# A list-scheduled attention and MLP kernel given a fixed order found by annealing, with one user at a time per PSUM bank and warm-up matmuls on a memset tile

## The chip, the cores and the metric

One core of a Trainium2 chip. Times are device microseconds (us) of one execution; where several executions were made, the median is given. The kernel before took 156.56 us (156.51 to 156.72, three runs). A profiled execution also has a **span**, from its first to its last instruction, about 2 us shorter than its time.

An execution can fall into a slower state, in which it takes over 1.5% longer than the fastest of the same kernel. Profiles whose execution was slow are named as such.

Engine names are those of the profile: PE does matmuls, DVE is the vector engine, ACT the scalar engine, POOL is GpSimd, SP issues most of the DMAs.

## The reference

An RWKV-style linear attention with a decaying state, then a LayerNorm and a two-layer MLP with a residual. Batch 4, 8 heads, 768 steps, head size 48; so 3072 rows of 384, which the kernel handles as 24 tiles of 128 rows.

```python
for t in range(S):                                   # per batch and head, D = 48
    cur   = einsum('bhd,bhe->bhde', u * k[t], v[t])
    y[t]  = einsum('bhd,bhde->bhe', r[t], state + cur)
    state = w * state + einsum('bhd,bhe->bhde', k[t], v[t])
x  = y, heads side by side                           # (4, 768, 384)
xn = (x - mean) / sqrt(var + 1e-6) * g_ln
out = x + maximum(xn @ w_ch1, 0) @ w_ch2             # 384 -> 1536 -> 384
```

## The kernel before

Each tile is a chain of some 20 tasks over all engines. r and k are scaled by powers of w on DVE or POOL (`scr`, `sck`), turned by PE (`TR`, `TK`) and evacuated by ACT or DVE (`rT`, `kT`). PE multiplies them (`at`), DVE masks (`A`), PE forms the bonus (`q`, `cc`, `cp`, `Vb`) and the state (`kv`, `S`, `Z`), then `y`. DVE adds (`x`), ACT or DVE centres (`xn`), the tile is turned (`ln`, `lc`, by PE for the first eight tiles and by DMA later), and PE does the MLP in pieces: three or six `up` with a relu each (`re`), three `dn`, then `ot` and the store `st`. The weights are scaled and cast on the way (`w1s`, `w2s`). `turn`, `vec`, `uw`, `wl` and `WLZ` prepare the decay and bonus vectors once.

A planner in the program walks these tasks with guessed costs and decides the order and, where there is a choice, the engine. Every engine then executes its own list in order.

```python
class Planner:
    def order(self, ...):
        ...
        while todo:
            for t in todo:                      # earliest start wins, then priority
                ...
                for eng, cost in [(t["eng"], t["cost"])] + (... t["alt"] or []):
                    ready = max(data, eng_at[eng] if eng else 0.0)
        ...
# (cut) one pool of PSUM, one bank per name, two for "hp":
#       at=1 (two banks), tr=1, s=1, y=1, hp=2, o=1
warm = ps.tile([P, 512], FP32, name="o")

def keep_warm(n):                               # matmuls that compute nothing
    for _ in range(n):
        nc.tensor.matmul(out=warm[:, :P], lhsT=ident[:], rhs=ident[:], start=True, stop=True)

def ln_transposes(i):
    ...
    tp_t[i] = ps.tile([P, 2 * HP, P], BF16, name="tr")     # shared with r and k transposes
    for kc in range(CK):
        nc.tensor.transpose(out=tp_t[i][:, kc, :], in_=xn_t[i][:, kc * P : (kc + 1) * P], identity=ident[:])
...
for t in plan.order():
    if t["eng"] == "PE":
        gap = t["start"] - pe_at - 0.1
        if gap > 0 and 0 not in o_t:            # where the plan leaves PE idle early on
            keep_warm(int(gap / 0.057))
        pe_at = t["start"] + t["cost"]
    ...                                         # emit t on the engine chosen
```

## Time and profile before

The profile that the prediction works from fell in the slow state. The kernel before was profiled again later, in a fast execution, with the same sources.

| kernel before | first profile (slow) | profiled again (fast) |
|---|---|---|
| time, us | 161.39 | 156.47 |
| span, us | 159.4 | 154.4 |
| mean granted PE clock | 0.989 | 1.000 |
| second half of `y` of tile 8 starts, us | 54.2 | 53.1 |
| end of PE, us | 156.15 | 151.15 |

How to read it: the activity rows give each engine's busy share in tenths, in 40 equal slices. The PE timeline gives the start of each group of matmuls, its length, and in brackets how long PE stood before it and for whom. The number to carry is the **lag**: the time at some place of the program less the useful PE work that stands before it (matmuls that the result needs, at full clock). It can only grow. Its last value, plus the 129 us of useful work and a tail after PE of some 3.25 us, is the span.

### The profile page before, as it was taken

To read this page: it belongs to the slowest core of one execution; us is meant where nothing else is said; L and a number is where in the kernel's file an instruction comes from. 1 tells how busy PE (TensorE), PEld (TensorE's weight loads), DVE (VectorE), ACT (ScalarE), POOL (GpSimd) and SP (SyncE) were. 2 spreads that over 40 slices of the span, in tenths; PEclk is the share of its full clock that TensorE was granted. 3 is DMA by queue.
4 is the path that set the end of the run, shared out by engine and by line. 5 is a ranking of instruction groups with operands and counts; after the bars stand their busy time and mean duration, and the time that the engine had idled before them with its cause. 6 is when DMAs were issued, how large, how long until landed. Compare 5 with 4: busy or idle time off the path is not lost.

```text
span 159.4 us, 4730 instructions
## 1 busy us (share of the span) xinstructions
PE 150.5 (94%) x1902; PEld 120.0 (75%) x1902; DVE 120.6 (76%) x246; ACT 94.2 (59%) x205; POOL 84.8 (53%) x115
## 2 busy tenths in 40 slices
PE   5999998999999999999999599999999999999991
PEld 5889887978887777677778367778787877777671
DVE  5879679699999999998899747779896965211142
ACT  3465787687868777677768444766767343354100
POOL 7387649486469857977988361874223622000000
PEclk9999999999999999999999968999999999999999
DMA  4999989998989998999586896211212122111122
GB/s 95 231 217 327 354 171 271 370 228 169 248 209 204 242 263 171 238 194 270 115 189 135 189 193 179 66 46 51 54 52 72 29 74 78 49 49 49 53 99 99
DMA packets 75563, 25.48 MB, mean 160 GB/s; under 512 B 69648, under 2 KB 74390, under 8 KB 75542
## 3 DMA queue, kind: packets, MB, share of 16 engines
q1 hardware_dynamic: 73542, 23.90, 62.1%
q10 hardware_dynamic: 1904, 1.28, 2.5%
q8 instruction: 15, 0.25, 0.6%
q14 instruction: 6, 0.05, 0.1%
q0 software_dynamic: 96, 0.01, 0.1%
HBM read 18.88 MB, written 4.72 MB: 148 GB/s over the span
## 4 chain that ended last, share of the span: by engine, by line
PE 55%; DVE 14%; SPq 14%; DMA 10%; issue 3%; ACT 1%; DVEq 0%; ACTq 0%
PE o L676 21%; PE hp L649 20%; SPq L212 9%; DMA wst<-in_moe_w_ch_dram 5%; DVE A L454 3%; DMA xT<-xn 3%; SPq L206 3%; PE at L444 2%; DMA k<-in_k_dram 2%; PE y L547 2%; PE tr L420 2%; PE tr L405 2%; DVE Z L519 2%; PE y L535 1%; SPq L234 1%
## 5 line engine op out<-in xcount | busy, mean ns | idle before, releaser
L649 PE MATMUL hp<-xT,w_sb 128*128 128x256 bf16 (+1 forms) x540 | 58.4, 253 | 2.4 <-DMA xT<-xn 2.0
L676 PE MATMUL o<-w_sb,hT 128*128 128x384 bf16 x264 | 52.9, 329 | 0.0
L663 ACT ACTIVATE hT<-hp 128x512 bf16<-128x512 f32 x62 | 36.5, 595 | 26.7 <-PE hp L649 26.1
L649 PEld LDWEIGHTS <-w_sb 128*128 128x128 bf16 x540 | 43.7, 98 | 10.5 <-DMA xT<-xn 2.4
L676 PEld LDWEIGHTS <-hT 128*128 128x128 bf16 x276 | 25.6, 98 | 11.9 <-issue 0.3
L454 DVE TENSOR_TENSOR A<-at,mask 128x1024 bf16<-128x1024 f32 x24 | 29.1, 1213 | 3.1 <-PE at L444 3.1
L479 POOL TENSOR_TENSOR Vb<-v,cc 128x384 f32<-128x384 f32 x24 | 21.2, 882 | 14.6 <-ACT cc L475 7.5
L686 DVE SCALAR_TENSOR_TENSOR ot<-o,rs,x 128x384 f32<-128x384 f32 x22 | 13.4, 610 | 16.2 <-PE o L676 16.0
L390 POOL TENSOR_TENSOR sc<-r,Fr 128x384 bf16<-128x384 f32 x15 | 16.3, 1094 | 4.1 <-DVE Fr L330 3.0
L387 POOL TENSOR_TENSOR sc<-k,Fk 128x384 bf16<-128x384 f32 x16 | 17.2, 1077 | 0.0
L587 ACT ACTIVATE sq<-x,sum 128x384 bf16<-128x384 f32 x24 | 14.7, 611 | 4.3 <-DVE x L560 3.1
L285 PE MATMUL o<-ident 128*128 128x128 bf16 x191 | 14.9, 236 | 1.6 <-DVE ident L260 1.6
L409 ACT COPY kT<-tr 128x512 bf16<-128x512 bf16 x22 | 12.8, 584 | 4.6 <-PE tr L405 2.7
L560 DVE SCALAR_TENSOR_TENSOR x<-y,Vb 128x384 f32<-128x384 f32 x24 | 13.1, 546 | 2.8 <-PE y L547 2.7
L285 PEld LDWEIGHTS <-ident 128*128 128x128 bf16 x191 | 12.7, 107 | 1.9 <-DVE ident L260 1.6
L426 ACT COPY rT<-tr 128x512 bf16<-128x512 bf16 x16 | 11.2, 738 | 2.9 <-PE tr L420 2.8
L598 POOL TENSOR_SCALAR rs<-sqs 128x2 f32<-128x2 f32 x12 | 2.5, 210 | 18.2 <-ACT sq L587 17.9
L574 DVE TENSOR_SCALAR xn<-x,sum 128x384 bf16<-128x384 f32 x17 | 10.0, 586 | 0.1
L405 PE MATMUL tr<-ident,sc 128*128 128x128 bf16 x92 | 9.1, 222 | 0.8 <-POOL sc L387 0.4
L444 PE MATMUL at<-rT,kT 48*128 48x128 bf16 x192 | 9.5, 218 | 0.3 <-ACT kT L409 0.2
L665 DVE TENSOR_SCALAR hT<-hp 128x512 bf16<-128x512 f32 x10 | 6.9, 685 | 3.0 <-PE hp L649 2.9
L601 POOL TENSOR_TENSOR rs<-rs,expo 128x2 f32<-128x2 f32 x12 | 8.6, 713 | 1.0
(93 smaller groups left out, 204.9 us busy)
## 6 DMA issues: line engine op xcount, KB each, us to landing
r<-in_r_dram SPq DMA_DIRECT2D x12, 384.0 KB, 4.9
k<-in_k_dram SPq DMA_DIRECT2D x24, 192.0 KB, 4.4
wst<-in_moe_w_ch_dram SPq DMA_DIRECT2D x6, 768.0 KB, 7.8
v<-in_v_dram SPq DMA_DIRECT2D x23, 192.0 KB, 4.2
out_dram<-ot SPq DMA_DIRECT2D x18, 192.0 KB, 2.2
out_dram<-ot ACTq DMA_DIRECT2D x5, 192.0 KB, 1.9
xT<-xn SPq DMA_TRANSPOSE x16, 2.6
v<-in_v_dram ACTq DMA_DIRECT2D x1, 192.0 KB, 3.8
```

Of the source, the lines that this page charges most:

```text
L212: eng.dma_start(out=dst[:], in_=src[b, :, s0 : s0 + L, :].rearrange("h t d -> t h d"))
L285: nc.tensor.matmul(out=warm[:, :P], lhsT=ident[:], rhs=ident[:], start=True, stop=True)
L387: eng.tensor_tensor(out=k_bufs[i % NSC][:, :, :D], in0=k_t[i][:], in1=Fk[:], op=ALU.mult)
L390: eng.tensor_tensor(out=r_bufs[e % NSR][:, j, :, :D], in0=r_t[e][:, :, j * D : (j + 1) * D], in1=Fr[:, j], op=ALU.mult)
L454: nc.vector.tensor_tensor(out=A_t[i][:].rearrange("p e q t -> p (e q) t"), in0=at_t[i][:].rearrange("p e q t -> p (e q) t"), in1=mask[:].u ...
L479: nc.gpsimd.tensor_tensor(out=Vb_t[i][:], in0=vf_t[i][:], in1=cc_t[i][:].unsqueeze(2).to_broadcast([P, H, D]), op=ALU.mult)
L560: nc.vector.scalar_tensor_tensor(out=x_t[i][:], in0=y_t[i][:, :C], scalar=1.0, in1=Vb_t[i][:].rearrange("p h d -> p (h d)"), op0=ALU.mult, ...
L587: nc.scalar.activation(out=sq[:], in_=x_t[i][:], func=ACT.Square, bias=sum_t[i][:], scale=-float(C), accum_out=sq_t[e][:, c : c + 1],)
L649: nc.tensor.matmul(out=hp[:, f * gw : (f + 1) * gw], lhsT=w1_sb[:, n, kc, fb * P : (fb + 1) * P], rhs=xT_t[g][:, kc, :gw], start=(kc == 0) ...
L663: nc.scalar.activation(out=out, in_=src, func=ACT.Relu)
L676: nc.tensor.matmul(out=o_t[i][:, :C], lhsT=hT_t[g][:, fk, j * P : (j + 1) * P], rhs=w2_sb[:, fk, :], start=(fk == 0), stop=(fk == FK - 1),)
L686: nc.vector.scalar_tensor_tensor(out=ot_t[i][:], in0=o_t[i][:, :C], scalar=rs_t[i // 2][:, i % 2 : i % 2 + 1], in1=x_t[i][:], op0=ALU.mult ...
```

## The change

The planner is no longer asked. A fixed list, found offline by annealing, gives the order of all tasks and the engine of each (`.A`, `.V`, `.G`, `.S` for ACT, DVE, POOL and SP; `*n` for n warm-up matmuls). The search modelled each PSUM bank as held by one user at a time. The transposes of the first four normalised tiles move from bank "tr" to bank "o". Warm-ups read a tile that DVE sets first of all, and the loads of r, k, v and the weights that had a choice between SP and ACT are all issued by SP. The intent is fewer waits in the first 50 us.

```diff
-SHIFT = { ... }                               # nudges for the planner
+ORDER = """
+r1 k1 k2 Fr0.V k3 v1 v2 w1l2 Fr1.A Fk.A w1l0 scr00.V scr10.G scr11.G r2 scr01.V *18 TR0 rT0.A sck0.V *1 TK0 kT0.A
+*1 turn vec uw.V rT1.A sck1.V vc0.V sck2.G *13 at0 *3 TK1 q0.V wl A0 *6 cc0 *1 kv0 kT1.A q1.G WLZ gn TR1 rT2.A *2
+y0 at1 rT3.A vc1.A cp0.V Vb0 Z0 sck3.G v3 A1 w1l1 TK2 kT2.V vc2.A cc1 cp1.A kv1 at2 x0 y1 xn0.A ln0 Vb1 q2.G Z1
+... (40 more rows)
+"""
     # (cut) Planner.order() now reads ORDER and only checks that each task follows what it needs
+    busy = const.tile([P, P], BF16, name="busy")
+    nc.vector.memset(busy[:], 1.0)
     ...
-            nc.tensor.matmul(out=warm[:, :P], lhsT=ident[:], rhs=ident[:], start=True, stop=True)
+            nc.tensor.matmul(out=warm[:, :P], lhsT=busy[:], rhs=busy[:], start=True, stop=True)
-    keep_warm(12)
+    keep_warm(18)
+    LNO = 4
+    def ln_bank(i):
+        return "o" if i < LNO else "tr"
     ...
-        tp_t[i] = ps.tile([P, 2 * HP, P], BF16, name="tr")
+        tl_t[i] = ps.tile([P, 2 * HP, P], BF16, name=ln_bank(i))
     # (cut) loads lose their choice of ACT; buffer reuse is written as explicit needs
-        gap = t["start"] - pe_at - 0.1         # no filling of gaps by the emission loop
-        ...
+        if "warm" in t:
+            keep_warm(t["warm"])
```

## The prediction

> **What bounds the kernel now.** I read the page first, then the PE timeline, then the DVE and DMA-queue timelines of the stretches that came out as limits.
>
> ```profile
> PE   5999998999999999999999599999999999999991
> ...
> DVE  5879679699999999998899747779896965211142
> ...
> PEclk9999999999999999999999968999999999999999
> DMA  4999989998989998999586896211212122111122
> ```
>
> Each digit is one fortieth of the span (4 us). PE looks full from the start, yet the row hides three things: warm-up matmuls, modelled overlaps, and one hole at slice 23 with a drop of the granted clock behind it. DVE is at 9 between slices 8 and 18 (32 to 76 us), and the DMA engines are full until about 90 us. The chain of waits says the same: DVE instructions carry it from 45 to 66 us, and from 92 us on it is PE alone, instruction after instruction. So there is a DVE-paced first half and a PE-paced second half.
>
> ```profile
> L649 PE MATMUL hp<-xT,w_sb 128*128 128x256 bf16 (+1 forms) x540 | 58.4, 253 | 2.4 <-DMA xT<-xn 2.0
> L676 PE MATMUL o<-w_sb,hT 128*128 128x384 bf16 x264 | 52.9, 329 | 0.0
> ...
> L454 DVE TENSOR_TENSOR A<-at,mask 128x1024 bf16<-128x1024 f32 x24 | 29.1, 1213 | 3.1 <-PE at L444 3.1
> ...
> L285 PE MATMUL o<-ident 128*128 128x128 bf16 x191 | 14.9, 236 | 1.6 <-DVE ident L260 1.6
> ```
>
> (The groups by line.) L285 is the 191 warm-up matmuls; they compute nothing. To see what PE really has to do I took starts of neighbouring pieces in the PE timeline: an "up" piece costs 0.66 us, a "down" piece 0.65, an r transpose 0.445, a k transpose 0.22, scores 0.33, bonus 0.105, state 0.17, y 0.20 and 0.17 more with carried state, an ln transpose 0.17, a half "down" 0.33. Times their counts (72, 69, 12, 24, 24, 24, about 24, 24/20, 8, 6): **129 us of useful PE work**. In this trace PE's useful work runs from 8.4 to 156.15 us. Define PE's **lag** at a moment as the time less the useful work already done; its final value sets the end.
>
> ```profile
> 27.94 0.33 PE L535 MATMUL y<-Z,rT 128*128 128x96 bf16 x4
> ...
> 45.62 0.36 PE L547 MATMUL y<-vv,A 128*128 128x48 bf16 x8
> ...
> 86.18 0.33 PE L535 MATMUL y<-Z,rT 128*128 128x96 bf16 x4
> ...
> 91.69 0.83 PE L649 MATMUL hp<-xT,w_sb 128*128 128x256 bf16 x6 [2.00 <-DMA xT<-xn]
> ...
> 93.40 1.49 PE L676 MATMUL o<-w_sb,hT 128*128 128x384 bf16 x4
> ```
>
> These are y of tiles 3, 6 and 15, then the hole and a "down" piece at half clock (0.65 us normally). Useful work before them in the order of the program: 10.6, 26.0, 64.4 us. Lag: **17.3, 19.6, 21.8**, and 27.1 at the end. Of the last 5.3, 2.0 is the wait and about 1.7 the half clock up to 96.7 us. This profiled run was slow (161.39 us, span 159.4, so 2.0 between the two); a fast run of 156.56 has a span of about 154.6, and a lag near 22.5. So nearly all lag is made **before 46 us**, not in the dense part.
>
> What makes it there: DVE. The same count for DVE (row means, less 0.05 us for the overlap of neighbours, since their sum exceeds the busy time by that) gives 35.0 us before y6 and 74.4 before y15. Time less DVE work: 8.9 at y3, 10.6 at y6, 11.8 at y15. DVE thus lost 2 to 3 us of waits up to y6, then hardly any.
>
> ```profile
> 16.73 0.48 DVE L371 TENSOR_SCALAR w_sb<-wst,g_neg 128x512 bf16<-128x512 f32 x1 [0.46 <-DMA wst<-in_moe_w_ch_dram]
> ...
> 20.68 0.74 DVE L426 COPY rT<-tr 128x512 bf16<-128x512 bf16 x1 [1.01 <-ACT rT L426]
> ...
> 31.50 0.36 DVE L381 CAST w_sb<-wst 128x384 bf16<-128x384 f32 x1 [1.37 <-DMA wst<-in_moe_w_ch_dram]
> ```
>
> (DVE timeline.) DVE, first in first out, stands at weight pieces that have not landed, and at one half of the r evacuation until ACT has read the other half of the same bank.
>
> **What the Trainium skill says.** *PSUM — Partial Sum Buffer*, section "PSUM bank collisions raise a hardware error", says two engines may not be in one bank and quadrant together, so software must order them. The trace agrees: DVE rT waits for ACT rT 3.1 us in 5 places. *SBUF — State Buffer*, "Who interferes with whom": a DVE instruction with two SBUF inputs contends with a GpSimd one that reads SBUF. The trace agrees: the same k scaling on DVE takes 1.14 us at 7.25, while GpSimd scales, and 0.54 at 40 us when GpSimd idles. *TensorE: Matmul & The Clock Gate*, "What's actually happening": PE starts at half clock and is released by activity. Warm-up matmuls start about 0.115 us apart at 1.61 us here and 0.057 later. *Perfetto Trace Analysis*, "Identifying the Most-Contended Engine", warns that matmul busy share misleads; here 94% stands over 129 useful us of 159.
>
> **The change part by part.**
> *Warm-ups.* 191 become 73 (in the built kernel: 18, 10 and 18 before the first r transposes, 27 later): 118 fewer at 0.057 is 6.7 us of PE time. But they filled waits, so alone they give at most the few tenths by which a useful piece stood behind one. The memset tile lets the first warm-up start about 0.5 us sooner; the start-up chain to the first transposes is DVE scans and PE table transposes, so 0 to 0.2 us.
> *Work per engine.* Useful PE work unchanged. DVE 119.3 to 116.7 us by row means, ACT 102 to 98, GpSimd 84 to 91. r evacuations on DVE fall from 8 to 4, xn from 17 to 12; relus on DVE rise from 10 to 18.
> *The order.* Useful PE / DVE work before y: y2 5.0/13.0 (was 7.9/15.5), y3 10.0/18.3 (10.6/19.0), y6 28.4/36.5 (26.0/35.0), y8 33.8/42.2 (34.0/43.6), y10 45.3/50.9 (46.6/56.4), y15 69.7/74.3 (64.4/74.4). By y15 PE has done 5.3 us more for the same DVE work. Adding what PE has left to the DVE work, the highest sum over all y is 139.1 before (at y15) and 137.7 after (at y4): 1.4 us, and DVE stops being a limit after y8.
> *Waits in the start.* r of the second pair is loaded and scaled first, so the rT2/rT3 wait (1.0 us) should vanish: both go to ACT well before q3. DVE's first W1 piece stands at 11.6 us of DVE work and belongs to the part now loaded first, so the 0.5 and 0.35 us waits go. Its first W2 piece stands at 23.0 rather than 21.3, about 29.7 us in time with an offset of 6.7; W2 lands from about 29.4, so most of the 1.37 us goes. Offset of DVE thus about 7 to 7.5 at y4 instead of 9.9.
> *Loads.* Up to the W2 loads the same bytes are asked for, in another order. Afterwards k, v and r arrive at some 206 GB/s (32 to 45 us), so k8 cannot land before about 41 us, where GpSimd would like it at 37. That eats part of the gain: I take an offset of 8.3 at y8 (10.3 before).
> Sum: y8 at 42.2 + 8.3 = 50.5 us, lag 50.5 - 33.8 = **16.7** (19.9 before). From there PE is the limit; before, lag grew by about 2.6 from y8 to the end of a fast run; I take 1.5 to 2 for small gaps, plus 0.7 for an xT wait (below). End of PE: 129.1 + 16.7 + 1.75 + 0.7 = 148.25. Tail 159.4 - 156.15 = 3.25, difference of run and span 2.0: 153.5. The same sum for before gives 129.1 + 22.5 + 5.25 = 156.85 against 156.56, and more waits in the start may go than the three I counted (0.84 at 9.2, 0.42 at 18 us, PE's own 0.4 twice, 1.3 us of warm-ups standing at 28.3 and 29.2 us). I credit 1.5 for those: **152.0 us**.
>
> **Rivals.**
> (a) *xT by DMA becomes the wait.* Useful PE work between y of a pair's last tile and its first "up" falls from 8.8, 8.7, 11.5 to 6.9, 6.7, 8.2 us for pairs 8/9, 10/11, 12/13. x, xn and the landing (median 2.6 us) need about 5, but the queue is in order: the transpose behind the hole was issued only at 86.91 and took 4.7 us. Each hole of 2 us also costs half clock. Two such holes: 155 to 156.
> (b) *The dense PE is all that counts and the start is DMA-bound:* then lag at y8 stays 19 and only the end improves: about 155.5.
> (c) *GpSimd, 7 us more, becomes a limit or slows DVE through the shared port:* its work before y14 rises from 57.6 to 62.5 us, with 82 us of time; it is in order, so late loads pass on. 1 to 2 us: about 153.5.
> (d) *The start improves fully:* lag 15 at y8: 150.
>
> **Range and chances.** Main line 152.0; (d) 149 to 150, (b) and (a) 155 to 156. Over 2% faster means below 153.4: the main line, (d) and part of (c), 0.70. Within 2%: 0.28. Slower needs several new holes, 0.02. Range 149.2 to 155.3.
>
> **What would show it.** Right: y8 near 50 us and y15 near 88; lag near 17 at y8 and under 19 at the end; DVE share from 32 to 76 us no longer all 9s; the chain on PE from some 50 us on; DVE rT no longer waiting for ACT. Wrong: y8 at 53 or later (start not repaired), or PE waits for xT over 1 us with a drop of the clock, or DVE still full at 70 to 86 us.

## The result, and the profile after

The changed kernel took **154.38 us** (153.73 to 154.83, four runs); the kernel before, run beside it, took 156.64 (156.51 to 159.13, one run of the four slow). The ratio of fast runs is **0.9855**, with a 95% interval of 0.981 to 0.9901. A ratio here and below is the mean time of one kernel's fast runs over that of the other's fast runs of the same rounds, so not quite the ratio of the medians. The outputs agree with the reference. The forecast was a gain of 4.6 us; the measured gain is 2.3, and the time lies inside the range of 149.2 to 155.3.

The profiled execution was a fast one: 154.30 us, span 152.5, mean clock 0.985. These are its rows for PE, DVE and the granted clock; a slice is 3.8 us.

```profile
PE   7959689999999999999999999999999999999991
...
DVE  5978999997799789899997897679889883535122
...
PEclk9995999999999999999999999999999999999998
```

The hole of the slow profile is gone. DVE is no longer at 9 in an unbroken row from 32 to 76 us. But a new dip stands at the front: counting slices from 0, the clock is at 5 in slice 3 (11.4 to 15.2 us), and PE is at 5, 6 and 8 in slices 2, 4 and 5, where the row of before had 9s. DVE is still at 9 in slices 18 to 20 (69 to 80 us), so one of the prediction's signs of being wrong, a DVE still full from 70 us on, is there in part. From the PE timeline, the place of that dip and the first half of `y` of tiles 8 and 15:

```profile
11.79 0.61 PE L381 MATMUL tr<-ident,sc 128*128 128x128 bf16 x4 [1.75 <-DVE sc L363]
...
51.10 0.33 PE L511 MATMUL y<-Z,rT 128*128 128x96 bf16 x4
...
88.35 0.33 PE L511 MATMUL y<-Z,rT 128*128 128x96 bf16 x4
```

PE stood 1.75 us for one k scaling on DVE. The same two `y` in the fast profile of the kernel before:

```profile
52.77 0.33 PE L535 MATMUL y<-Z,rT 128*128 128x96 bf16 x4
...
85.09 0.33 PE L535 MATMUL y<-Z,rT 128*128 128x96 bf16 x4
```

Tile 15 comes later because the new order puts 5.3 us more PE work ahead of it, so start times alone mislead; the lag does not. It is counted here at the second half of `y` (some 0.2 us after the lines above), less the useful work before that piece:

| lag, us | y0 | y2 | y5 | y8 | y15 | end of PE |
|---|---|---|---|---|---|---|
| before (slow profile) | | 16.4 | 19.9 | 20.4 | 22.2 | 26.9 |
| before (fast profile) | 10.1 | 15.6 | 18.8 | 19.3 | 21.1 | 21.9 |
| changed | 12.3 | 15.0 | 17.4 | 17.6 | 19.0 | 20.0 |
| changed, second profile | 11.4 | 14.7 | 16.6 | 16.8 | 18.1 | 19.2 |
| changed, third profile | 12.0 | 14.7 | 16.8 | 17.0 | 18.4 | 19.4 |

(The fast profile of before and the last two rows come from runs told further down. The prediction's own lags count the piece of `y` itself as done and are so 0.4 us lower: its 16.7 at tile 8 is 17.1 in this table.)

Three things are seen. The new order is **behind** at y0 by 2.2 us, catches up by y2, and is ahead by 1.7 at y8 (in the other two profiles by 0.9 at y2 and by 2.3 to 2.5 at y8). From y8 to the end both grow alike: 2.6 before, 2.4 in all three profiles after. So what was won was won before 51 us. And the end is 19.2 to 20.0, close to what the prediction's sum had without its last term.

What bounds the kernel in the first 32 us changed its kind. In the chain of waits of the kernel before (fast profile), columns start, length and what, the stretch up to 30 us is a DMA queue and then one load:

```profile
22.73 7.63 DMA wst<-in_moe_w_ch_dram
...
30.38 0.36 DVE w_sb L381
```

In the chain of the changed kernel DVE has taken that place, one instruction behind the other:

```profile
23.50 1.13 DVE A L430
24.62 0.27 DVE xT L619
24.89 0.60 DVE hT L648
25.49 0.65 DVE w_sb L347
26.14 0.65 DVE rT L402
```

The stretches of time say by how much. Each line is a stretch: its bounds and length, then busy us of PE, PE's weight loads, DVE, ACT and POOL with the number of instructions, the granted clock, DMA share and GB/s. First before (fast profile), then changed:

```profile
12.00:16.00 4.00, 4.00 (x85) 3.77 (x82) 4.00 (x10) 2.05 (x7) 2.99 (x5) 1.00 1.01 373
20.00:32.00 12.00, 11.65 (x210) 10.40 (x208) 10.54 (x22) 9.34 (x21) 8.77 (x12) 1.00 1.04 290
```

```profile
12.00:16.00 4.00, 3.44 (x48) 3.29 (x47) 3.48 (x7) 2.69 (x6) 3.37 (x4) 0.65 0.95 302
20.00:32.00 12.00, 11.57 (x213) 10.23 (x209) 11.96 (x23) 8.74 (x20) 9.92 (x13) 1.00 0.94 277
```

From 12 to 16 us the clock is 0.65 instead of 1.00. From 20 to 32 us DVE rises from 10.54 to 11.96 of 12 us: the wait for a load is gone and DVE is full. That repeats: all three profiles of the changed kernel have 11.96. The DMA share does not (0.94, 1.07 and 1.07), and nothing is read from it.

The hole begins on DVE (DVE timeline of the changed kernel, bonus weights and the k scaling behind them):

```profile
8.85 1.54 DVE L327 TENSOR_TENSOR uwI<-vec 48x4 bf16<-48x4 f32 x2
10.42 1.31 DVE L363 TENSOR_TENSOR sc<-k,Fk 128x384 bf16<-128x384 f32 x1
```

and on POOL at the same time:

```profile
8.42 1.95 POOL L366 TENSOR_TENSOR sc<-r,Fr 128x384 bf16<-128x384 f32 x2 [4.68 <-DMA r<-in_r_dram]
```

Two multiplications of 48x4 took 1.54 us; in the kernel before, where POOL was at the small power `wl` at that moment, they took 0.33. The k scaling took 1.31 us instead of the 0.55 of the one at 7.2 us, when POOL stood. The first ran beside the scaling of r of the second pair on POOL, which the new order puts first and for which POOL had waited 4.68 us; the second beside POOL's next instruction, a k scaling from 10.33 us. That POOL is the cause is so far only argued; an experiment below (s_wl) moves its work.

### The profile page after: what moved, and what is told of

Same layout as the page of the kernel before. It is cut to its first block, busy times and chain, and to the rows that moved or that the text cites.

```text
span 152.5 us, 4495 instructions
## 1 busy us (share of the span) xinstructions
PE 143.7 (94%) x1784; PEld 112.5 (74%) x1784; DVE 120.3 (79%) x247; ACT 89.1 (58%) x198; POOL 90.0 (59%) x122
## 4 chain that ended last, share of the span: by engine, by line
PE 71%; DVE 17%; DMA 3%; ACT 3%; issue 2%; POOL 1%; ACTq 0%; POOLq 0%; DVEq 0%
PE o L659 26%; PE hp L632 25%; PE at L420 4%; DMA rows<-in_u_dram 3%; DVE A L430 3%; PE tr L381 3%; PE tr L396 3%; PE y L523 2%; PE s L471 2%; DVE hT L648 2%; DVE x L536 2%; PE y L511 2%; DVE sc L363 1%; DVE q L413 1%; ACT rT L402 1%
## 5 line engine op out<-in xcount | busy, mean ns | idle before, releaser
L646 ACT ACTIVATE hT<-hp 128x512 bf16<-128x512 f32 x54 | 32.0, 599 | 22.2 <-PE hp L632 21.6
L659 PEld LDWEIGHTS <-hT 128*128 128x128 bf16 x276 | 24.5, 97 | 10.5 <-issue 0.2
L366 POOL TENSOR_TENSOR sc<-r,Fr 128x384 bf16<-128x384 f32 x19 | 19.7, 1045 | 8.4 <-DMA r<-in_r_dram 8.4
L385 ACT COPY kT<-tr 128x512 bf16<-128x512 bf16 x19 | 11.1, 586 | 13.0 <-PE tr L381 10.0
L402 ACT COPY rT<-tr 128x512 bf16<-128x512 bf16 x20 | 13.9, 744 | 4.4 <-PE tr L396 2.6
L648 DVE TENSOR_SCALAR hT<-hp 128x512 bf16<-128x512 f32 x18 | 12.3, 684 | 4.0 <-PE hp L632 3.8
L363 POOL TENSOR_TENSOR sc<-k,Fk 128x384 bf16<-128x384 f32 x13 | 13.6, 1049 | 0.3 <-DMA k<-in_k_dram 0.3
L495 POOL TENSOR_TENSOR Z<-S,WLZ 128x384 bf16<-128x384 f32 x9 | 9.0, 1004 | 7.8 <-DVE S L486 7.8
L574 POOL TENSOR_SCALAR rs<-sqs 128x2 f32<-128x2 f32 x12 | 2.5, 207 | 18.1 <-ACT sq L563 17.5
L381 PEld LDWEIGHTS <-sc 128*128 128x128 bf16 x96 | 6.4, 99 | 4.4 <-DVE sc L363 2.6
L554 ACT ACTIVATE xn<-x,sum 128x384 bf16<-128x384 f32 x12 | 7.4, 615 | 2.6 <-DVE x L536 2.4
```

Source lines behind the costliest of these rows:

```text
L363: eng.tensor_tensor(out=k_bufs[i % NSC][:, :, :D], in0=k_t[i][:], in1=Fk[:], op=ALU.mult)
L366: eng.tensor_tensor(out=r_bufs[e % NSR][:, j, :, :D], in0=r_t[e][:, :, j * D : (j + 1) * D], in1=Fr[:, j], op=ALU.mult)
L381: nc.tensor.transpose(out=tk_t[i][:, q, :], in_=sc[:, q, :], identity=ident[:])
L402: (eng.copy if eng is nc.scalar else eng.tensor_copy)(out=rT_t[i][:].rearrange("p q (t j) -> p q j t", j=2), in_=tp_t[e][:, :, c * LH : (c ...
L646: nc.scalar.activation(out=out, in_=src, func=ACT.Relu)
L648: nc.vector.tensor_scalar(out=out, in0=src, scalar1=0.0, scalar2=None, op0=ALU.max)
```

## The experiments

Sixteen runs were made, some of them of unedited kernels, in four calls, each call on one chip with the kernel before beside it. The kernel before was slower and more scattered than at first: medians of 157.29, 157.21, 157.48 and 157.84, with fast runs from 156.5 to 159.3. The changed kernel stayed within 153.6 to 154.8 throughout. So ratios are compared only within one call, or against the changed kernel's own absolute time. All sixteen outputs agree with the reference; a "pad" is an extra multiplication whose result nobody reads. Starts of `y` (y0, y2, ...) are those of its second half, as in the table.

Theories at the start. **T1:** the new hole at 10 to 12 us, with the half clock behind it, ate the prediction's last credit. **T2:** DVE paces 19 to 38 us whatever happens before. **T3:** the bank move gave the gain, not the order. **T4:** the warm-up tile did.

### The changed kernel again (after_again)

No edit.

> The changed kernel unchanged, as the measure for the other three on this chip. Both theories: ratio to the kernel before 0.985, within 0.981 to 0.990; the trace shows the PE wait of 1.7 us before the k transposes of tile 1 near 10 us and half clock to 15 us again.

It took 153.96 us (153.63 to 154.5, six runs), ratio 0.9784 (0.9749 to 0.9819). The ratio is below the range expected. The clock of its profiled run was 0.978, and the hole was there again (1.63 us), but the half clock came later, at 13.4 us, and lasted to 20.2. So the hole is a property of the kernel, while when the half clock follows is not fixed by it, and the 0.9855 and this differ mostly by the kernel before (156.64 there, 157.29 here).

### Take the hole away, by order (s_sck1, s_wl)

```diff
 s_sck1:
-... kT0.A *1 turn vec uw.V rT1.A sck1.V vc0.V ...
+... kT0.A sck1.V *1 turn vec uw.V rT1.A vc0.V ...
 s_wl, in addition to it:
-scr00.V scr10.G scr11.G r2 scr01.V ... sck2.G *13 at0 *3 TK1 q0.V wl A0
+scr00.V r2 scr01.V ... uw.V wl scr10.G scr11.G rT1.A vc0.V sck2.G *13 at0 *3 TK1 q0.V A0
```

> One move: DVE scales k of tile 1 before it copies the row vector and makes uw, in the 0.9 us in which it stood idle. Theory A (the gain was lost to a new hole in the start: PE waits 1.7 us for this scaling, then runs at half clock for 3 us, and DVE, which carries the chain until 34 us, is late by as much): the wait falls under 0.5 us, y of tile 0 starts at 13.2 instead of 14.4 us, y of tile 8 at 50 instead of 51.1, and the time falls by 0.8 to 1.5 us against the changed kernel. Theory B (the stretch of 20 to 45 us is bound by loads and DVE work in any case, so a hole before it is swallowed): y of tile 3 stays within 0.4 us of 25.6 and the time within 0.4 us.

> The same move, and GpSimd makes the decay power before it scales r of the second pair, so that uw on DVE (1.54 us beside GpSimd scaling, 0.34 us in the kernel before) runs alone. Theory A: uw takes 0.4 us, no PE wait over 0.5 us before 16 us, no half clock after 10 us, y of tile 0 near 12.3 us, y of tile 8 near 49.3, and 1.5 to 2.5 us less than the changed kernel. Theory B: within 0.4 us of it.

s_sck1: 153.82 us, 0.9769 (0.9728 to 0.9809). s_wl: 154.42 us, 0.981 (0.9773 to 0.9847). Neither can be told from 0.9784. The k scaling is early in both, but s_sck1 did not take the hole away: PE now stands 1.82 us for the bonus product `q`, until 12.58 us. In s_wl no wait of PE from 9 to 20 us is over 0.8 us. The half clock went in neither, against the expectation for s_wl: it ran from 15 to 21.5 us in s_sck1 and from 16.3 to 23 us in s_wl.

s_wl shows what had made DVE slow. With the scaling of r out of the way, the same DVE instructions take 0.56 and 0.34 us (DVE timeline of s_wl):

```profile
9.08 0.56 DVE L363 TENSOR_TENSOR sc<-k,Fk 128x384 bf16<-128x384 f32 x1 [1.33 <-DMA k<-in_k_dram]
...
9.75 0.34 DVE L327 TENSOR_TENSOR uwI<-vec 48x4 bf16<-48x4 f32 x2
```

In s_sck1, where POOL still scales r at that moment, the two multiplications took 1.72. Yet y2 is at 19.7 (s_sck1) and 19.6 us (s_wl) against 19.6 in the run without edit. What holds y1 and y2 now is read in the chain of waits. In s_sck1 it is ACT, which does in order two r evacuations, two casts, and only then the small bonus copy that PE waits for (and behind that PE itself, busy without a gap from 16 to 20 us at clock 0.50):

```profile
13.56 1.33 ACT rT L402 x2
...
14.91 0.93 ACT vv L372 x2
15.84 0.07 ACT cc L451
```

In s_wl it is POOL, whose list was pushed back by the scaling of r:

```profile
13.71 1.15 POOL q L413
14.85 0.79 POOL Vb L455
15.64 0.96 POOL sc L363
```

So the cause of the hole is shown, and taking away the wait alone gains nothing: behind it stand two other chains of almost the same length, on ACT and on POOL. Since the half clock stayed, these two runs do not yet decide T1; the next one does.

### Keep the hole, fill it (c_warm)

```diff
-*13 at0 *3 TK1 q0.V
+*13 at0 *31 TK1 q0.V
```

> 28 more warm-up matmuls in the hole of the changed kernel, nothing else: the wait stays, the clock should stay full. Theory A says wait and clock both cost: about 0.5 to 1 us less than the changed kernel, y of tile 0 at 13.7 instead of 14.4 us. Theory B: within 0.3 us.

It took 153.48 us, 0.9762 (0.9724 to 0.98). PE now has warm-ups to do while it waits (PE timeline):

```profile
9.68 1.91 PE L261 MATMUL o<-busy 128*128 128x128 bf16 x31
11.88 0.40 PE L381 MATMUL tr<-ident,sc 128*128 128x128 bf16 x4 [0.29 <-DVE sc L363]
```

The clock row of this kernel is 9 throughout. Against after_again, y2 moves from 19.6 to 19.0 us. But y5 is at 38.4 (38.2 there) and y8 at 50.6 (50.4), with a lag of 17.0 at y8 and 19.3 at the end: what is won at y2 is gone by y5. The gain in time, 0.2%, lies within the intervals. So T1 falls: the hole and its half clock delay y2 by some 0.6 us and cost nothing that can be measured at the end.

### The kernel before again (base)

No edit to the kernel before, one look.

> The kernel before, unchanged, for a profile that is not in the slow state. If the hole at 89.5 us with half clock behind it belongs to the slow executions only, PE waits under 0.5 us in one place after 46 us, and the lag of PE grows by 2 to 3 us from y of tile 8 to the end. If it belongs to all, the hole of about 2 us is there again and the span is 156 or more.

156.47 us, span 154.4, clock 1.000, no PE wait over 0.3 us after the first warm-up. So the hole and the half clock at 90 us of the first profile belonged to a slow execution, and no term of the gain may be drawn from them. Its lags stand in the table above. At 156.47 it is as fast as any run of this kernel.

### Is DVE the limit at 19 to 38 us? (p_early, d_relu, v_pool)

p_early adds four pads on DVE in that stretch:

```diff
+nc.vector.tensor_tensor(out=pad[:], in0=Fr[:, 0], in1=Fk[:], op=ALU.mult)
# once each after lc2, sck4, x3 and Z3
```

d_relu takes four relus off DVE and gives them to ACT; v_pool takes four weight and k pieces off DVE and gives them to POOL:

```diff
 d_relu:
-re1_2.V ... re0_1.V ... re2_2.V ... re1_1.V
+re1_2.A ... re0_1.A ... re2_2.A ... re1_1.A
 v_pool:
-w1s11.V ... sck4.V ... w2s12.V (after re3_2) ... w2s21.V (after up4_0)
+w1s11.G ... sck4.G ... w2s12.G (after w2s11)  ... w2s21.G (after w2s20)
```

> The changed kernel with four useless DVE multiplications (some 0.5 to 0.8 us each, so 2 to 3 us) spread over its work from 22 to 32 us. Theory B1 (from 19 to 34 us DVE is full and paces everything, which is why holes before it cost nothing): y of tile 5 starts 1.5 to 2.5 us later than 38.2 to 39.0 and the time rises by as much, to about 156. Theory B2 (that stretch is paced by loads): DVE has room, under 0.5 us more.

> Four relus between 24 and 31 us (0.68 us each on DVE) go to ACT, which is busy 8.7 of 12 us from 20 to 32 us. Theory B1: y of tile 5 earlier by 1 to 2 us, time 0.7 to 2 us less than the changed kernel. Theory B2: within 0.4 us. A miss on the other side: ACT, in order, makes k or r evacuations late, and it gets slower.

> Theory B1 (DVE paces from 19 to 38 us), tested by taking work off DVE without making anything late: four of its instructions (a W1 piece, k of tile 4, two W2 pieces; 0.65 + 0.65 + 0.3 + 0.3 = 1.9 us net) go into gaps in which GpSimd waits, 26.7 to 28.5 and 33.1 to 34.5 us. B1: y of tile 5 starts 0.8 to 1.7 us earlier than 38.2 to 39.0, the time falls by 0.7 to 1.5 us against the changed kernel, to 152.5 to 153.3. If the stretch is bound elsewhere (loads, or the shared port gives it back): within 0.4 us.

p_early: 156.27 us, 0.9956 (0.9921 to 0.9992). The pads took 0.54 to 1.44 us each, and the lag at y4 went from 16.5 (16.9 on record) to 18.4, and at the end from 19.2 (20.0) to 21.7. Some 3 us of DVE work cost about 2 us of the end. That supports T2. It is not proof by itself, since pads later on cost nearly as large a share (p_late below: 155.66 against 156.27).

d_relu: 158.43 us, 1.0076 (1.0051 to 1.0101). It takes work off the engine that paces, yet it cost some 4 us. ACT is in order too, and now everything behind the relus came late to PE (PE timeline):

```profile
29.60 0.38 PE L380 MATMUL tr<-ident,sc 128*128 128x128 bf16 x4 [1.30 <-ACT rT L401]
...
32.18 0.34 PE L606 MATMUL o<-ident,xn 128*128 128x128 bf16 x3 [0.86 <-ACT xn L553]
```

The lag at y5 was 21.2 instead of 16.6. ACT is busy only 8.74 of 12 us in this stretch, so a busy share does not tell whether an engine can take more: what counts is whose turn comes when.

v_pool: 154.21 us (153.15 to 155.48, one of six runs slow; 154.07 over the other five), 0.9766 (0.972 to 0.9813). In its profile DVE falls from 11.96 to 11.23 of 12 us from 20 to 32 us, the lag at y5 is 15.9 instead of 16.6 to 17.4, and 18.8 at the end instead of 19.2 to 20.0; the hole (1.65 us) and a half clock (17 to 20 us) are still there. So T2 is borne out in the trace: less work on DVE brings y5 forward by what was expected. The times scatter too much to tell the kernel from the changed one.

### Is DVE still a limit later? (p_late, b_plate)

The same four pads between 60 and 77 us, after x9 to x12, in the changed kernel (p_late) and in the kernel before (b_plate):

```diff
 p_late: ORDER
-... x9 up6_4 ... x10 S10 ... x11 q13 ... x12 ot7 ...
+... x9 (pad) up6_4 ... x10 (pad) S10 ... x11 (pad) q13 ... x12 (pad) ot7 ...
 b_plate: emission loop of the kernel before
+            if t["name"] in ("x9", "x10", "x11", "x12"):
+                nc.vector.tensor_tensor(out=pad[:], in0=Fr[:, 0], in1=Fk[:], op=ALU.mult)
```

> The same four multiplications after the x of tiles 9 to 12, from about 60 to 75 us, where the changed order should have left DVE room. Prediction's step (DVE stops being a limit after y8): under 0.5 us more. If DVE still paces there: 2 us more.

> The kernel before with the same four useless DVE multiplications after the x of tiles 9 to 12 (60 to 77 us). It has DVE full in that stretch, so it should lose as much as they take or more: 2 to 2.5 us over the kernel before. The changed kernel lost 1.5 to 1.7. If it loses under 1 us, DVE did not pace the kernel before there, and my reading of it was wrong.

p_late: 155.66 us, 0.9896 (0.9871 to 0.9921), so 1.3 to 1.7 us over the changed kernel's medians. b_plate: 159.26 us, 1.0085 (1.0035 to 1.0136), 1.3 us over the kernel before by the ratio, less than the 2 to 2.5 expected. The pads came to 2.75 us. In p_late's DVE timeline one of them stands right ahead of the bonus product `q`,

```profile
70.74 1.09 DVE L876 TENSOR_TENSOR pad<-Fr,Fk 128x384 bf16<-128x384 f32 x1
71.76 0.41 DVE L416 TENSOR_TENSOR q<-rT,tr 128x512 bf16<-128x512 bf16 x1
```

and PE stands for that `q`, because `q` reads the PSUM bank into which the next transposes must go:

```profile
72.31 0.61 PE L399 MATMUL tr<-ident,sc 128*128 128x128 bf16 x8 [1.25 <-DVE q L416]
```

The lag goes from 17.6 at y10 to 19.9 at y12, where it grows by 0.8 without pads. So DVE is a limit after y8 as well, in both kernels (it is busy 15.66 of the 17 us from 60 to 77 before, and 16.09 in the changed kernel), though it is not the bound in the sum over the whole stretch: an order that is fixed has little slack at any one place.

### Bank and warm-up tile, undone one at a time (u_bank, u_ident), and done alone (o_old)

```diff
 u_bank:  -    LNO = 4
          +    LNO = 0
 u_ident: -... lhsT=busy[:], rhs=busy[:] ...
          +... lhsT=ident[:], rhs=ident[:] ...
 o_old:   ORDER holds the old kernel's order, engines and early warm-ups, word for word;
          LNO = 3, warm-ups on the memset tile, none after the first normalised transposes
```

> The changed kernel with one part undone: the ln transposes of tiles 0 to 3 back in the bank of the k and r transposes. The order was made with the other bank in mind; four more users of that bank between 18 and 34 us. Expected: PE or the copies wait some tenths more, 0.3 to 1 us slower. If the bank is nothing: within 0.3 us.

> The changed kernel with the warm-ups reading the identity again. The first warm-up starts 0.57 us later (1.61 against 1.04 us), the table transposes at 4.4 us may run colder (1.76 us for six before, 1.37 after). Expected: start of y of tile 0 later by 0.2 to 0.5 us, and, since DVE paces later, 0 to 0.3 us on the time.

> The new parts with the old order: the order of the kernel before written out as the fixed table, memset warm-ups (none after the first ln transposes, as the bank is then taken), ln transposes of tiles 0 to 2 in the o bank (tile 3 would deadlock there in that order). If the order makes the gain and the bank only keeps it possible: within 0.5 us of the kernel before. If the bank by itself is worth the 1.7 us that undoing it cost: 1 to 1.7 us less than the kernel before.

u_bank: 156.15 us, 0.9887 (0.9837 to 0.9937), against 0.9766 and 0.9778 of two kernels with the bank move: 1.1%, or 1.7 us, is lost. PE stands for the evacuation of the normalised tile before it may use "tr" again:

```profile
19.73 0.59 PE L381 MATMUL tr<-ident,sc 128*128 128x128 bf16 x4 [0.99 <-DVE xT L619]
```

and y2 is at 21.2 instead of 19.6 us. (In this profile the half clock lasted from 12.4 to 22.7 us, longer than in the others; how much of the loss is that, no run separates.) u_ident: 153.99 us, 0.9778 (0.9736 to 0.982): the tile that warm-ups read makes no difference that can be measured. T4 falls. Its later warm-ups also left a hole of only 0.94 us, and the clock of that profile stayed at 1.000.

o_old: 158.76 us (156.81 to 163.05, three of six runs slow; 157.66 over the fast three), 0.9969 (0.9895 to 1.0043); its profile was slow, so nothing is read from it. (With the bank of all four tiles moved, the old order would deadlock: its fourth transposes stand between two `dn` pieces of tile 0, which hold "o" until the last of them; so three were moved.) The bank move gives nothing measurable in the old order, though with three fast runs a gain of up to 1% is not excluded, and three tiles are not four. It is worth 1.7 us in the new order, and the new order without it still gains 1.1% (u_bank, 0.9837 to 0.9937). So T3 in its strict form falls: the order gains something alone, and about half of the whole gain needs order and bank together.

### The changed kernel a third time, and two versions made from these findings (after_third, v_best, v_cp)

v_best is v_pool with c_warm's filled hole. v_cp is v_pool with the k scaling early as in s_sck1, the filling put elsewhere, and the bonus copy of tile 1, which ACT held up, on DVE:

```diff
 v_best = v_pool and:  -*13 at0 *3 TK1        +*13 at0 *31 TK1
 v_cp   = v_pool and:  -uw.V rT1.A sck1.V     +sck1.V *1 turn vec uw.V rT1.A
                       -wl A0 *6 cc0          +wl A0 *32 cc0
                       -cc1 cp1.A             +cc1 cp1.V
```

> The changed kernel again, as the measure on this chip for the other three; ratio to the kernel before 0.978 to 0.985.

> The changed kernel with the hole at 10 us filled by warm-ups (full clock, y of tile 2 0.7 us earlier) and the four moves from DVE to GpSimd (y of tile 5 0.7 to 1 us earlier). If the two act one after the other, as the reading says (first the start up to y2, then DVE from 19 to 38 us): y of tile 5 at 36.8 to 37.5 us, lag at the end 18 to 18.6, and 1 to 1.6 us less than the changed kernel. If one swallows the other: 0.5 us less.

> The same with k of tile 1 scaled before uw, the warm-ups moved to the hole that this opens before the first bonus, and the bonus copy of tile 1 on DVE, as ACT does it only after two r evacuations and two casts (15.8 us). If ACT in order is what sets y2 once the hole is gone: y of tile 2 at 18.5 instead of 19.1, and 0.3 to 0.6 us less than the kernel before it in this list. If the GpSimd chain (dense from 8.4 to 18.5 us) sets it: no difference.

Changed kernel: 154.32 us, 0.9769 (0.9718 to 0.9819). **v_best: 153.23 us** (152.93 to 154.09), **0.9708** (0.9659 to 0.9758). v_cp: 153.31 us, 0.9714 (0.966 to 0.9769). v_best beats the kernel before by over 2%. It is ahead of the changed kernel by 0.6%, 1.1 us by the medians; the two intervals overlap, though the runs hardly do (152.93 to 154.09 against 153.79 to 154.60), so this last step is likely rather than settled. c_warm and v_cp, at most 0.25 us above it, pass 2% as well. The profile of v_best supports it: y2, y5 and y8 lag 14.0, 15.9 and 16.2, the end 18.6, and in its chain of waits the stretch that had been a load, then DVE, is now PE:

```profile
22.89 0.67 PE hp L632 x12
23.56 0.45 PE tr L396 x8
24.01 0.78 PE hp L632 x12
24.79 0.17 PE y L511 x4
```

In the same 12 us as before, PE is at 11.99 and DVE no longer full (v_pool, without the filling, had 11.97 and 11.23):

```profile
20.00:32.00 12.00, 11.99 (x222) 10.89 (x223) 11.06 (x24) 8.96 (x20) 11.13 (x15) 1.00 1.00 306
```

Nearly all of this is v_pool's: the filling moves y5 by 0.1 us and the end of PE by 0.2.

v_cp brings nothing more. It does not clear ACT's bonus copy: on DVE the copy came at 15.93 us, later than at 15.62 on ACT in v_best, and PE waited 0.74 us for it.

## Why the prediction was wrong in its size

The mechanism was the predicted one in the main: a better start, and the same dense part after it. What was off is in the main one term of the sum. In the order of its steps:

- **The bound before.** Right: nearly all the lag is made before 46 us (18.8 of 21.9 at y5 in the fast profile). From a slow profile it estimated a lag of 22.5 at the end of a fast run; it is 21.9. (In the rows that it shows DMA is at 8 or 9 only up to 76 us, not to 90, and it counts the slice of the hole from 1 and the others from 0; neither enters the sum.)
- **Warm-ups and their tile.** The tile: 0 to 0.2 us expected, nothing measured (u_ident). The removed warm-ups were expected to give a few tenths. They also **cost** something that the prediction did not count: the old ones had kept PE running through the start (4.00 of 4 us and clock 1.00 from 12 to 16), and without them one wait of 1.75 us was followed by half clock. By c_warm that is 0.6 us at y2 and nothing at the end.
- **Work per engine.** Right for ACT (93.8 us busy before, 89.1 after) and POOL (84.9 and 90.0). Wrong for DVE, which was to have 2.6 us less: it is busy 120.3 us before and 120.3, 121.0 and 119.7 after. Its new list is cheaper at the old row means, but in the new order several rows take longer, as the two 48x4 multiplications do.
- **Waits in the start.** Right for those named: in the list of DVE's waits, 2.8 us for ACT's half of the r evacuation and 1.4 us for a weight load (fast profile of before) have no counterpart after, and the load is gone from the chain.
- **y8 at 50.5 us.** Right: 51.3, 50.4 and 50.7 in three profiles. **y15 near 88:** right, 88.5, 87.7 and 87.9.
- **Growth to the end of 2.45.** Right within 0.4: on the table's count it is 2.05 and was 2.4. The 0.7 us put aside for an xT wait was not used by one; rival (a) did not happen.
- **"DVE stops being a limit after y8."** Wrong as a statement: 2.75 us of pads there cost 1.3 to 1.7. It did no harm to the number, since the growth was the same before and after. It came from a sum over whole stretches, which is blind to single places.
- **Bank move.** It got no term. It is worth 1.7 us to this order (u_bank, half clock included) and nothing measurable to the old one (o_old), so no term of its own was due, though the prediction did not say why.
- **The credit of 1.5 us for further waits in the start. This is the step that failed.** It took for granted that the other small waits of the start would vanish and lower the lag by as much. With the credit the lag at y8 should have been 15.6 on the table's count, without it 17.1; it was 17.6, 16.8 and 17.0, so none of the credit arrived. Two things came instead. A new hole of 1.75 us with half clock after it put y0 1.3 to 2.2 us further behind than before; but filling it (c_warm) left y8 at 17.0, so it is not what ate the credit. What stood behind was DVE, full from 20 to 32 us (11.96 of 12): pads of 3.1 us there cost 2 us (p_early), and 1.9 us of work taken off it brought the lag at y8 to 16.3 (v_pool). So time saved ahead of that stretch is spent in it; the pads and the trace of v_pool support this, though the times of v_pool alone do not settle it. The prediction counted DVE's offset at y4 and y8, but in the credit it treated waits before that stretch as if they added to the lag one for one.

The sum for the profiled run closes: 152.0, plus the 1.5 not received, plus 0.5 (lag 17.6 instead of 17.1 at y8), plus 0.35 (growth), plus 0.1 (129.2 us of work), less 0.2 (1.8 instead of 2.0 between span and time), is 154.25; it took 154.30. Without the credit the prediction's sum is 153.5, and the three medians of the changed kernel are 154.38, 153.96 and 154.32.

Of the rivals, (b) said that the lag at y8 stays 19 and only the end improves; the reverse was seen. (c), at 153.5, came closest in its number: POOL did slow DVE, at the very start, and in s_wl POOL in order was the chain. But taking the slowing away (s_wl) gained nothing, so that its number is near is luck as far as the runs show. (d) needed a lag of 15 at y8 (15.4 on the table's count), which not even v_best reached (16.2).

How much of the credit was to be had at all? v_best, which fills the hole and takes four pieces off DVE, is 1.1 us faster by the medians, but by relieving DVE and not by the waits that the credit named. No run shows that those could have given it.

**Still open:** what holds y2 in v_best and v_cp (their lag there, 14.0 and 14.2, is three quarters of the total); why v_pool's fast runs scatter over 1.5 us; when an idle PE is put on half clock; and how much of u_bank's loss is the bank and how much the longer half clock.

## What to carry to other kernels

Do not credit a reordering with waits that you have not followed to what stands behind them: when one wait goes, the next chain of nearly equal length takes over (here load, then DVE, and with DVE relieved at last PE). A repair ahead of an engine that is full later on can be swallowed there (0.6 us at y2 and nothing left at y5 in c_warm), so follow it to the end of that stretch. A busy share or a count of work over a long stretch says nothing about slack at one place of a fixed order: test it with a few microseconds of useless work on the engine in question. Before removing filler matmuls, look at what wait they stand in: here half clock followed once they were gone.

## What the Trainium skill lacked or had wrong

- *TensorE: Matmul & The Clock Gate*, section "What's actually happening", has the clock go down after at least one idle window of about 3.4 us. Here shorter idle stretches were followed by half clock: in the three profiles of the changed kernel one wait of 1.6 to 2.0 us from about 10 us on, with half clock from 11.5, 13.4 and 12.5 us; in v_pool, with 1.65 us, only from 17 us. The spells of half clock lasted 3.4 us (the changed kernel and its third profile, v_pool), 6.7 (its second, s_sck1) or 10.3 (u_bank), so the length of the window fits; the idle time that it takes does not. In s_wl no single wait in the 7 us before the half clock was over 0.8 us; PE was busy 2.16 of the 4 us from 12 to 16, and the clock was 0.56 from 16 to 20. With the hole filled by 28 matmuls the clock stayed at 9 in every slice (c_warm). The measurement decides; what share of a window PE must stand idle, no page says and no run here settles. (The clock that a profile shows is not exact either: it reads 1.00 for 0 to 4 us, where the first warm-up matmuls start 0.113 us apart and later ones 0.057.)
- *SBUF — State Buffer*, section "Who interferes with whom", says that a DVE instruction with two SBUF inputs contends with a POOL instruction that reads SBUF. The runs agree for large POOL instructions: two 48x4 multiplications on DVE took 1.54 us beside POOL's scaling of r and 0.34 with that moved away (s_wl). They also took 0.33 and 0.34 beside POOL's `wl`, which reads only 4 values per partition from SBUF and shows 1.04 us (base, s_wl; spans of POOL are rough). So the length shown of the POOL instruction does not say how long it holds DVE, and the section gives no way to tell.
- *Perfetto Trace Analysis*, section "Identifying the Most-Contended Engine", warns against PE's busy share and takes occupancy as a fair measure for the other engines. ACT at 8.74 of 12 us could not take four relus of about 0.6 us without costing the kernel some 4 us (d_relu), and DVE pads of 2.75 us cost 1.3 to 1.7 us in a stretch where the whole-stretch count gave DVE slack (p_late). No page says how to judge slack under a fixed order per engine.
